# Attention followed by a spatially gated MLP in float32 on one core: fixed PSUM banks for the scores and for the product with v, and one combined wait ahead of each piece

## The chip, the cores and the metric

The kernel runs on one core of one Trainium2 chip. The metric is device time in microseconds (us), lower is better. The profile is of one execution on the same core.

## What is computed

Eight batches of eight heads, 576 positions, head width 64. Attention has a decay between positions, a causal mask and a softmax; its output, with the heads side by side, goes through a gated MLP whose gate mixes the positions.

```python
scores = scale * np.matmul(q, k.transpose(0, 1, 3, 2))          # scale = 1/8
cum = np.cumsum(np.log(np.clip(f, 0.0001, 1.0)), axis=-1)
scores = np.where(causal, -1000000000.0, scores + cum[:, :, :, None] - cum[:, :, None, :])
attn = np.exp(scores - np.max(scores, axis=-1, keepdims=True))
attn = attn / (np.sum(attn, axis=-1, keepdims=True) + 1e-09)
x = np.matmul(attn, v)                                          # then (batch, position, 512)
h = np.maximum(x @ w_in, 0.0)
u, v = h[..., :512], h[..., 512:]
v_n = (v - np.mean(v)) / np.sqrt(np.var(v) + 1e-06)             # mean and variance over the last axis
v_s = np.einsum('ts,bsd->btd', w_spatial, v_n) + b_spatial[None, :, None]
out = (u * v_s) @ w_out
```

## The kernel before, in words

**Attention works on pairs of heads.** There are 32 pairs, four to a batch (`attention`, from L366). For a pair P the matrix engine (PE) does five kinds of work, all of it in float32:

- `scores` (L241): for each block i of 128 query rows, and for each of the two heads h, one product of 64 rows of the array, n = 128(i+1) columns wide, into a PSUM tile `sc`. The two heads lie on partitions 0-63 and 64-127, so that the two products of a block use the two halves of the array's rows. The products are issued in two **pieces** (L246): blocks 2, 1, 0 (L258, called the **small piece** below: widths 384, 256, 128) and block 3 alone (the **wide piece**: width 512). Blocks 0 and 1 of a head share a tile.
- `scores_tail` (L282): the last 64 query rows of both heads, two products of 288 columns (L289, listed under L196, the line of the helper `mm`).
- `transposes` (L320) and `transposes_tail` (L335): the softmaxed rows `tt` and `tl` are turned, 128x128 at a time, into PSUM tiles `tp` (L325 and L336) and copied into `e` alternately by VectorE (DVE) and ScalarE (ACT) (`evac`, L316).
- `attend` (L343): the **product with v**, one piece of 28 matmuls on half of the array's columns each (L352), into two `sc` tiles, x0 and x1.

Every float32 product of L258, L196 (`sc`) and L352 is two instructions in the profile (x2 for one product).

**Between them** DVE adds the decay to the scores, takes the row minimum and writes `tt` (`lowest`, L235, listed under L238); ACT takes the exponential (L271); DVE inverts the row sums (L274, L275); GpSimd (POOL) scales the rows (L279); then they are transposed. `tt` exists once for each head, `tl` once, `e` twice.

**PSUM.** The `sc` tiles come from a pool of four buffers (L521, L535), the `tp` tiles from one of two; two more (`ps`) take the MLP's sums. A new `sc` tile waits for the last reader of the tile that lay there before it.

**What sets the order.** Two Python generators, attention and the MLP of a batch (`moe`, L403), are stepped in turn (L538 to L546), so that the attention of batch b+1 runs beside the MLP of batch b. A scheduler then orders each engine's queue: of the instructions that it holds ready in its own model of time it takes the one with the highest priority. `in_one_piece` (L183) ties the matmuls of a piece together: each after the first has a high priority and an ordering (no semaphore) behind the one ahead of it. The first matmul of a piece is tied to its own tile alone. So the scheduler may start a piece when the first tile is free, and put other matmuls between its members while a later tile is not. Each engine works through its queue strictly in that order.

**The two stages of the run.** Up to about 100 us the weights are loaded and split into two float32r parts (`load64`, L112, on DVE, ACT and POOL) beside the four pairs of batch 0. Then the MLP of batch 0 starts beside pair 4, and so on.

```python
        for piece in ((0, 1, 2), (3,)):
            ...
                    if i == 1:
                        at[i, h] = at[0, h][0], 128
                    else:
                        at[i, h] = PS['s'].tile([128, 512], F32, name="sc"), 0
            ...
            in_one_piece([product(i, h) for i in reversed(piece) for h in range(2)])
```

Of the kernel before, what the change touches and what calls it, by code (L numbers as in the profile page):

```python
# [31 lines left out]
def f32(ap):  # L32
    return ap.bitcast(F32)
# [3 lines left out]
def attn_gmlp_kernel(ctx: ExitStack, tc: tile.TileContext, qk, v, f, w_in, w_sp, b_sp, w_out, out):  # L37
# [141 lines left out]
    def behind(i, j):  # L179
        tc.add_manual_dep(i.ins, j.ins.name, mybir.DependencyInfo(  # L180
            mybir.DependencyClass.NoSync, mybir.DependencyReason.DATA), reason="order")

    def in_one_piece(jobs):  # L183

        was = None
        for n, job in enumerate(jobs):
            if was is None:
                was = job()
            else:
                with tc.high_priority():  # L190
                    i = job()
                behind(i, was)
                was = i

# [40 lines left out]
    def lowest(out, ps, dec, acc_):  # L235
        if len(dec.shape) == 3:
            out, ps = (a.rearrange("p (c w) -> p c w", c=2) for a in (out, ps))
        V.tensor_tensor_reduce(out=out, in0=ps, in1=dec, scale=-0.125, scalar=3.0e38, op0=ALU.add, op1=ALU.min,  # L238
                               accum_out=acc_)

    def scores(P):  # L241
# [4 lines left out]
        for piece in ((0, 1, 2), (3,)):  # L246
            at = {}
            for i in piece:
                for h in range(2):
                    if i == 1:  # L250
                        at[i, h] = at[0, h][0], 128
                    else:
                        at[i, h] = PS['s'].tile([128, 512], F32, name="sc"), 0
# [11 lines left out]
            for i in reversed(piece):  # L265
                for h in range(2):
                    ps, c = at[i, h]
                    n = 128 * (i + 1)
                    t = tt[h][:, TOFF[i]:TOFF[i] + n]
                    lowest(t, ps[:, c:c + n], decay(dk[h], i), nm[h][:, i:i + 1])  # L270
                    last["exp", P, h, i] = A.activation(t, t, AF.Exp, bias=nm[h][:, i:i + 1], scale=-1.0,  # L271
                                                        accum_out=sm[h][:, i:i + 1])
# [9 lines left out]
    def scores_tail(P):  # L282
# [3 lines left out]
        for j in range(2):  # L286
            k0 = 288 * j
            sc = PS['s'].tile([128, 512], F32, name="sc")
            mm(sc[:, 0:288], qk_t[:, TL:640], qk_t[:, 640 + k0:928 + k0], True, True)  # L289
            lowest(tl[:, k0:k0 + 288], sc[:, 0:288], dt[:, k0:k0 + 288], nm[:, j:j + 1])  # L290
            if P == 0:
                keep_warm(6)
            yield 485
        V.tensor_tensor(out=nm[:, 2:3], in0=nm[:, 0:1], in1=nm[:, 1:2], op=ALU.min)
# [21 lines left out]
    def evac(out, ps):  # L316
        (V.tensor_copy if nev[0] % 2 == 1 else A.copy)(out, ps)  # L317
        nev[0] += 1

    def transposes(P, h):  # L320
        for c in range(NB):
# [6 lines left out]
            evac(e_tile(P)[:, h, e0:e0 + n], tp[:, 0:n])  # L328
            yield 107 * (NB - c)

    def transposes_tail(P):
        for cs, off, step in (((4, 3), 576, 640), ((0, 1, 2), 512, 512)):
# [7 lines left out]
            evac(bass.AP(tensor=st.tensor, offset=st.offset,  # L340
# [3 lines left out]
    def attend(P, xh, xl):  # L344

        vt, e = vts[P], es.pop(P)
        x0, x1 = (PS['s'].tile([128, 512], F32, name="sc") for _ in range(2))
# [10 lines left out]
        in_one_piece(jobs)  # L358
        yield 2950
        for ps, s0, n in ((x0, 0, 256), (x1, 256, 320)):  # L360
            last[P, s0 // 256] = A.copy(xh[:, s0:s0 + n], ps[:, 0:n])
            V.tensor_tensor(out=xl[:, s0:s0 + n], in0=ps[:, 0:n], in1=f32(xh[:, s0:s0 + n]), op=ALU.subtract)
# [34 lines left out]
    def acc(b):  # L397

        nps[0] += 1
        pool, tag = ((ps_m, "ps"), (PS["t"], "tp"), (PS["s"], "sc"))[nps[0] % 3 if b == B - 1 else 0]  # L400
# [120 lines left out]
    with tc.tile_pool(name="ws", bufs=2) as ws, tc.tile_pool(name="p0s", bufs=4, space=PSUM) as p0s, \  # L521
# [13 lines left out]
    for k, n in (("s", 4), ("t", 2)):  # L535
# [54 lines left out]
```

## Time and profile before

| | |
|---|---|
| time, median of 3 runs | 825.17 us (824.89 to 825.52) |
| the profiled execution's own time | 830.26 us, its span 828.5 us |
| PE busy | 802.9 us, 97% of the span |
| DVE, ACT, POOL busy | 441.5, 408.2, 387.2 us |
| PE's idle time ahead of L258 in the whole span | 6.6 us |
| PE's idle time ahead of L352 | 2.6 us |
| mean granted PE clock | 0.97 |

A row of a group or of the timeline gives the line, the engine, the operation, what it writes and reads (`sc<-qk_t`), the part of the array (64\*128 is half of the rows, 128\*64 half of the columns) and how many instructions (x4). In the timeline the first number is the start, the second the length; neighbouring matmuls overlap by their pipeline, so what one costs is the distance to the start of the next one.

### The profile page before, as it was taken

The page shows a single profiled execution, that of the slowest core. Times are in us where ns is not written, and L with a number is a line of the kernel's source. Part 1 is how long each engine was busy: PE and PEld are TensorE (multiplying, and loading weights), DVE is VectorE, ACT ScalarE, POOL GpSimd, SP SyncE. Part 2 cuts the span into 40 slices and gives each one's busy share as a digit, 9 for nine tenths or more (in the row PEclk, how much of TensorE's full clock was granted, in tenths as well). Part 3 has the DMA queues.
Part 4 walks back from the last instruction along what each step waited for, and adds up shares of the span by engine and source line. Part 5 has one row for each costly group of instructions (what it writes and reads, how often), then busy time and mean ns, then how long its engine had stood idle before and what let it go on. Part 6 is the DMA issues. An engine that isn't in the chain of part 4 may idle for free.

```text
span 828.5 us, 14548 instructions
## 1 busy us (share of the span) xinstructions
PE 802.9 (97%) x4934; PEld 620.8 (75%) x4934; DVE 441.5 (53%) x1482; ACT 408.2 (49%) x1092; POOL 387.2 (47%) x703
## 2 busy tenths in 40 slices
PE   8888889999999999999999999999999999999997
PEld 3444567877788878887778877888678877888896
DVE  6886687444555546455654446445463445543321
ACT  3565565445654545445554355544454445643321
POOL 4797685443544336444444337344444435432221
PEclk9578899999999999999999999999999999999999
DMA  7563721233222232233212332222222332201001
GB/s 241 174 188 108 218 86 57 82 118 119 76 88 74 85 116 90 93 118 105 74 53 89 102 131 93 87 95 92 72 91 79 118 118 83 61 25 43 26 1 64
DMA packets 35213, 79.44 MB, mean 96 GB/s; under 512 B 4161, under 2 KB 8257, under 8 KB 35138
## 3 DMA queue, kind: packets, MB, share of 16 engines
q1 hardware_dynamic: 34818, 77.98, 29.7%
q8 instruction: 39, 0.64, 0.3%
q10 hardware_dynamic: 320, 0.52, 0.2%
q14 instruction: 36, 0.29, 0.1%
HBM read 68.73 MB, written 9.75 MB: 95 GB/s over the span
## 4 chain that ended last, share of the span: by engine, by line
PE 85%; POOL 1%; issue 0%; DVE 0%; ACT 0%; POOLq 0%
PE ps L196 47%; PE sc L258 11%; PE sc L352 10%; PE tp L325 8%; PE sc L196 5%; PE tp L196 2%; PE tp L336 2%; POOL tt L279 0%; POOL vnl L439 0%; POOL mv L434 0%; POOL w L126 0%; POOL wol L128 0%; ACT o L508 0%; ACT vx L430 0%; DVE st L431 0%
## 5 line engine op out<-in xcount | busy, mean ns | idle before, releaser
L279 POOL TENSOR_SCALAR tt<-tt,sm 128x128 f32<-128x128 f32 (+3 forms) x256 | 134.8, 545 | 154.5 <-DVE sm L275 110.0
L271 ACT ACTIVATE tt<-tt,nm 128x384 f32<-128x384 f32 (+3 forms) x256 | 142.6, 558 | 99.1 <-DVE nm L238 86.6
L258 PE MATMUL sc<-qk_t 64*128 64x128 f32 (+3 forms) x512 | 123.3, 481 | 6.6 <-DVE nm L238 6.3
L325 PE MATMUL tp<-ident,tt 128*128 128x128 f32 x640 | 113.0, 287 | 2.4 <-POOL tt L279 2.4
L317 DVE COPY e<-tp 128x384 f32<-128x384 f32 (+1 forms) x160 | 71.0, 447 | 70.8 <-PE tp L325 56.0
L317 ACT COPY e<-tp 128x256 f32<-128x256 f32 (+1 forms) x160 | 71.4, 450 | 71.8 <-PE tp L325 45.5
L325 PEld LDWEIGHTS tp<-ident,tt 128*128 128x128 f32 x640 | 78.9, 145 | 36.6 <-POOL tt L279 6.7
L484 POOL TENSOR_TENSOR gl<-u,gh 128x256 fp32r<-128x256 f32 (+1 forms) x64 | 51.3, 802 | 107.3 <-ACT gh L483 107.1
L352 PE MATMUL sc<-e,vraw 128*64 128x320 f32 (+4 forms) x896 | 95.4, 365 | 2.6 <-DVE e L317 2.6
L352 PEld LDWEIGHTS sc<-e,vraw 128*64 128x64 f32 x896 | 60.1, 138 | 40.9 <-DVE e L317 4.8
L238 DVE CUSTOM_DVE_ANT_1 tt<-sc,dk 128x256 f32<-128x256 f32 (+1 forms) x128 | 70.3, 552 | 36.6 <-PE sc L258 22.3
L258 PEld LDWEIGHTS sc<-qk_t 64*128 64x128 f32 x512 | 55.0, 191 | 38.8 <-issue 15.2
L196 PE MATMUL ps<-xh,winh 128*128 128x256 f32 (+1 forms) x232 | 74.0, 319 | 2.6 <-ACT vx L430 2.6
L196 PE MATMUL ps<-sph,vnh 128*128 128x256 f32 (+1 forms) x240 | 76.4, 318 | 0.0
L196 PE MATMUL ps<-spl,vnh 128*128 128x256 f32 (+1 forms) x240 | 71.8, 299 | 0.0
L196 PE MATMUL ps<-sph,vnl 128*128 128x256 f32 (+1 forms) x240 | 71.4, 297 | 0.0
L196 PE MATMUL ps<-xl,winh 128*128 128x256 f32 (+1 forms) x232 | 70.7, 305 | 0.0
L196 PE MATMUL ps<-xh,winl 128*128 128x256 f32 (+1 forms) x232 | 70.2, 303 | 0.0
L238 DVE CUSTOM_DVE_ANT_0 tt<-sc,dk 128x128 f32<-128x128 f32 (+1 forms) x128 | 53.4, 419 | 22.5 <-PE sc L258 12.9
L196 PE MATMUL ps<-winh,xh 128*128 128x512 f32 x148 | 61.5, 416 | 0.0
L196 PE MATMUL ps<-winl,xh 128*128 128x512 f32 x148 | 59.5, 402 | 0.0
L483 ACT CAST gh<-u 128x256 fp32r<-128x256 f32 (+1 forms) x64 | 27.6, 433 | 58.1 <-DVE u L480 41.5
(165 smaller groups left out, 1681.7 us busy)
## 6 DMA issues: line engine op xcount, KB each, us to landing
dk<-rows_d SPq DMA_DIRECT2D x64, 320.0 KB, 3.5
qk_t<-in_dram SPq DMA_DIRECT2D x32, 608.0 KB, 3.8
vraw<-in_dram SPq DMA_DIRECT2D x32, 320.0 KB, 3.0
dt<-rows_d SPq DMA_DIRECT2D x64, 144.0 KB, 3.2
out_dram<-o SPq DMA_DIRECT2D x32, 256.0 KB, 2.8
w<-in_dram SPq DMA_DIRECT2D x8, 512.0 KB, 5.8
w<-in_dram SPq DMA_DIRECT2D x8, 256.0 KB, 3.5
wraw<-in_dram SPq DMA_DIRECT2D x4, 288.0 KB, 5.7
```

Source lines behind the costliest of these rows:

```text
L196: T.matmul(o, l, r, start=st, stop=sp)
L238: V.tensor_tensor_reduce(out=out, in0=ps, in1=dec, scale=-0.125, scalar=3.0e38, op0=ALU.add, op1=ALU.min, accum_out=acc_)
L258: return lambda: T.matmul(ps[:, c:c + n], qk_t[p, n - 128:n], qk_t[p, 640:640 + n], start=True, stop=True)
L271: last["exp", P, h, i] = A.activation(t, t, AF.Exp, bias=nm[h][:, i:i + 1], scale=-1.0, accum_out=sm[h][:, i:i + 1])
L279: G.tensor_scalar(out=t, in0=t, scalar1=sm[h][:, i:i + 1], scalar2=1.0, op0=ALU.mult, op1=ALU.mult)
L317: (V.tensor_copy if nev[0] % 2 == 1 else A.copy)(out, ps)
L325: T.transpose(out=tp[:, (i - c) * 128:(i - c + 1) * 128], in_=tt[h][:, TOFF[i] + 128 * c:TOFF[i] + 128 * c + 128], identity=ident)
L336: T.transpose(out=tp[:, j * 128:(j + 1) * 128], in_=tl[:, c * 128:(c + 1) * 128], identity=ident)
L352: return lambda: T.matmul(x[64 * h:64 * h + 64, q0 - s0:q1 - s0], vt[:, c, h, :], e[:, h, e0 + q0:e0 + q1], start=c == 0, stop=c == end)
L483: A.copy(gh[j][:, 0:nt], g)
L484: G.tensor_tensor(out=gl[j][:, 0:nt], in0=g, in1=f32(gh[j][:, 0:nt]), op=ALU.subtract)
```

## The change

Four things are changed.

- **Fixed banks.** The pool of four `sc` buffers becomes four tags, `sc0` to `sc3`, of one buffer each (`bank`). The small piece has banks 0 and 1 for blocks 0 and 1 of the two heads, and banks 2 and 3 for block 2. The wide piece has banks 0 and 1, the tail 2 and 3, the product with v 0 and 1. The MLP of the last batch takes the four in turn.
- **One wait ahead of a piece.** `freed` holds the last reader of each bank. The first matmul of a piece depends, with a semaphore, on the readers of all the banks that the piece has asked for.
- **The product with v** depends besides on all ten copies into `e` of its pair (`copied`), where before each matmul waited for the copies that it reads.
- `lowest` and `evac` return or keep their instructions for this; their work is the same.

The matmuls, their number and their shapes are the same; no instruction is added on DVE, ACT or POOL.

```diff
-    def behind(i, j):
+    def behind(i, j, sync=False):
         tc.add_manual_dep(i.ins, j.ins.name, mybir.DependencyInfo(
-            mybir.DependencyClass.NoSync, mybir.DependencyReason.DATA), reason="order")
-
-    def in_one_piece(jobs):
+            mybir.DependencyClass.Sync if sync else mybir.DependencyClass.NoSync, mybir.DependencyReason.DATA),
+            reason="order")
+
+    freed, banks = {}, []
+
+    def bank(n):
+
+        t = PS['s'].tile([128, 512], F32, name="sc", tag=f"sc{n}")
+        banks.append(n)
+        return t
+
+    def in_one_piece(jobs, needs=()):
 
         was = None
-        for n, job in enumerate(jobs):
+        for job in jobs:
             if was is None:
                 was = job()
+                for j in [freed[n] for n in banks if n in freed] + list(needs):
+                    behind(was, j, sync=True)
             else:
                 with tc.high_priority():
                     i = job()
                 behind(i, was)
                 was = i
+        banks.clear()
...
-                    if i == 1:
-                        at[i, h] = at[0, h][0], 128
-                    else:
-                        at[i, h] = PS['s'].tile([128, 512], F32, name="sc"), 0
+                    at[i, h] = (at[0, h][0], 128) if i == 1 else (bank(i % 3 + h), 0)
...
-                    lowest(t, ps[:, c:c + n], decay(dk[h], i), nm[h][:, i:i + 1])
+                    freed[i % 3 + h if i != 1 else h] = lowest(t, ps[:, c:c + n], decay(dk[h], i), nm[h][:, i:i + 1])
...
-            sc = PS['s'].tile([128, 512], F32, name="sc")
+            sc = bank(2 + j)
             mm(sc[:, 0:288], qk_t[:, TL:640], qk_t[:, 640 + k0:928 + k0], True, True)
-            lowest(tl[:, k0:k0 + 288], sc[:, 0:288], dt[:, k0:k0 + 288], nm[:, j:j + 1])
+            freed[2 + j] = lowest(tl[:, k0:k0 + 288], sc[:, 0:288], dt[:, k0:k0 + 288], nm[:, j:j + 1])
...
-    def evac(out, ps):
-        (V.tensor_copy if nev[0] % 2 == 1 else A.copy)(out, ps)
+    copied = {}
+
+    def evac(P, out, ps):
+        copied.setdefault(P, []).append((V.tensor_copy if nev[0] % 2 == 1 else A.copy)(out, ps))
         nev[0] += 1
...
-        x0, x1 = (PS['s'].tile([128, 512], F32, name="sc") for _ in range(2))
+        x0, x1 = bank(0), bank(1)
...
-        in_one_piece(jobs)
+        in_one_piece(jobs, copied.pop(P))
...
-            V.tensor_tensor(out=xl[:, s0:s0 + n], in0=ps[:, 0:n], in1=f32(xh[:, s0:s0 + n]), op=ALU.subtract)
+            freed[s0 // 256] = V.tensor_tensor(out=xl[:, s0:s0 + n], in0=ps[:, 0:n], in1=f32(xh[:, s0:s0 + n]),
+                                               op=ALU.subtract)
...
-        pool, tag = ((ps_m, "ps"), (PS["t"], "tp"), (PS["s"], "sc"))[nps[0] % 3 if b == B - 1 else 0]
+        k = nps[0] % 3 if b == B - 1 else 0
+        pool, tag = ((ps_m, "ps"), (PS["t"], "tp"), (PS["s"], f"sc{nps[0] // 3 % 4}"))[k]
...
-    for k, n in (("s", 4), ("t", 2)):
+    for k, n in (("s", 1), ("t", 2)):
```

The order of the queues is made anew by the scheduler. Three places of PE's queue show it. In these rows `sc<-qk_t` of widths 384 to 128 is the small piece, of width 512 the wide one, of 288 the tail; `tt_82` and `tt_83` are the rows of the first and the second head, transposed into `tp`; rows of `ps` are the MLP's; x2 are the products of the two heads one behind the other. After the change the helper's line L196 is L208, L258 is L267, L325 is L337, L336 is L348 and L352 is L364.

The first place is the small piece of a pair in the middle of the run. Before:

```order
L258 MATMUL sc<-qk_t 128x384 x2
L258 MATMUL sc<-qk_t 128x256
L196 MATMUL ps<-winh,xl 128x512
L196 MATMUL ps<-winh,xh 128x512
L196 MATMUL ps<-winl,xh 128x512
L196 MATMUL ps<-winh,xl 128x512
L196 MATMUL ps<-winh,xh 128x512
L258 MATMUL sc<-qk_t 128x256
L258 MATMUL sc<-qk_t 128x128 x2
```

The same piece of the changed kernel:

```order
L267 MATMUL sc<-qk_t 128x384 x2
L267 MATMUL sc<-qk_t 128x256 x2
L267 MATMUL sc<-qk_t 128x128 x2
L208 MATMUL ps<-winh,xh 128x512
L208 MATMUL ps<-winl,xh 128x512
L208 MATMUL ps<-winh,xl 128x512
```

The piece is whole: no row of the MLP stands between the 256-wide products of the two heads any more. All small and all wide pieces of the changed kernel stand so.

The second place is the end of a pair, from its last transposes to the product with v. Before, the wide piece of the next pair stands 17 rows ahead of these:

```order
L336 MATMUL tp<-ident,tl 128x128 x2
L196 MATMUL ps<-woh,gl 128x512
L196 MATMUL sc<-qk_t 128x288
L196 MATMUL ps<-woh,gh 128x512
L196 MATMUL ps<-wol,gh 128x512
L196 MATMUL ps<-woh,gl 128x512
L336 MATMUL tp<-ident,tl 128x128 x3
L196 MATMUL ps<-woh,gh 128x512
L196 MATMUL ps<-wol,gh 128x512
L196 MATMUL ps<-woh,gh 128x512
L196 MATMUL ps<-wol,gh 128x512
L325 MATMUL tp<-ident,tt_82 128x128 x4
```

Now:

```order
L267 MATMUL sc<-qk_t 128x512 x2
L337 MATMUL tp<-ident,tt_83 128x128
L348 MATMUL tp<-ident,tl 128x128 x2
L208 MATMUL sc<-qk_t 128x288
L208 MATMUL ps<-woh,gh 128x512
L208 MATMUL ps<-wol,gh 128x512
L208 MATMUL ps<-woh,gh 128x512
L208 MATMUL ps<-wol,gh 128x512
L208 MATMUL ps<-woh,gl 128x512 x2
L348 MATMUL tp<-ident,tl 128x128 x3
L337 MATMUL tp<-ident,tt_82 128x128 x2
```

The wide piece of the next pair has moved back, to ten rows ahead of the first transposes of that same pair (`tt_82`), which need what DVE, ACT and POOL make of it.

The third place is in the first stage, the wide piece of pair 2. Before, with the product with v of pair 1 behind it:

```order
L258 MATMUL sc<-qk_t 128x512
L325 MATMUL tp<-ident,tt_83 128x128 x3
L258 MATMUL sc<-qk_t 128x512
L325 MATMUL tp<-ident,tt_83 128x128 x7
L196 MATMUL sc<-qk_t 128x288 x2
L336 MATMUL tp<-ident,tl 128x128 x5
L352 MATMUL sc<-e,vraw 64x320 x2
```

Now:

```order
L337 MATMUL tp<-ident,tt_83 128x128 x7
L208 MATMUL sc<-qk_t 128x288
L348 MATMUL tp<-ident,tl 128x128 x5
L267 MATMUL sc<-qk_t 128x512 x2
L364 MATMUL sc<-e,vraw 64x320 x2
```

The wide piece is whole and stands behind all transposes of the pair ahead of it; the product with v, which takes the same two banks, follows on its heels.

More of the change, by code (lines that the diff above doesn't have):

```diff
@@ L237, in lowest @@
             out, ps = (a.rearrange("p (c w) -> p c w", c=2) for a in (out, ps))
-        V.tensor_tensor_reduce(out=out, in0=ps, in1=dec, scale=-0.125, scalar=3.0e38, op0=ALU.add, op1=ALU.min,
+        return V.tensor_tensor_reduce(out=out, in0=ps, in1=dec, scale=-0.125, scalar=3.0e38, op0=ALU.add, op1=ALU.min,
                                accum_out=acc_)
@@ L293, in scores_tail @@
             yield 485
+        banks.clear()
         V.tensor_tensor(out=nm[:, 2:3], in0=nm[:, 0:1], in1=nm[:, 1:2], op=ALU.min)
@@ L327, in transposes @@
             e0 = EOFF[c]
-            evac(e_tile(P)[:, h, e0:e0 + n], tp[:, 0:n])
+            evac(P, e_tile(P)[:, h, e0:e0 + n], tp[:, 0:n])
             yield 107 * (NB - c)
@@ L339, in transposes_tail @@
             st = e_tile(P)[:, :, off:off + 64]
-            evac(bass.AP(tensor=st.tensor, offset=st.offset,
+            evac(P, bass.AP(tensor=st.tensor, offset=st.offset,
                          ap=[list(st.ap[0]), [step, n], list(st.ap[1]), list(st.ap[2])]), pv)
@@ L519, in step @@
             return round(done), False
-    with tc.tile_pool(name="ws", bufs=2) as ws, tc.tile_pool(name="p0s", bufs=4, space=PSUM) as p0s, \
+    with tc.tile_pool(name="ws", bufs=2) as ws, tc.tile_pool(name="p0s", bufs=1, space=PSUM) as p0s, \
             tc.tile_pool(name="p0t", bufs=4, space=PSUM) as p0t:
```

## The prediction

> **What bounds the kernel now.** I read the page first, then busy time by stage, the waits of the matrix engine (PE), and PE's timeline around the pieces that the change touches. The page's PE row:
>
> ```profile
> PE 802.9 (97%) x4934; PEld 620.8 (75%) x4934; DVE 441.5 (53%) x1482; ACT 408.2 (49%) x1092; POOL 387.2 (47%) x703
> ```
>
> PE is the only full engine, but 97% is a mean over two stages. Busy time by stretch (PE, weight loads, DVE, ACT, POOL, then PE's granted clock):
>
> ```profile
> 0.00:127.00 127.00, 107.14 (x487) 64.72 (x488) 97.68 (x286) 71.12 (x188) 89.94 (x141) 0.81 0.55 168
> 127.00:826.00 699.00, 695.71 (x4450) 556.12 (x4448) 343.81 (x1197) 337.06 (x904) 297.31 (x562) 1.00 0.26 83
> ```
>
> From 127 us on PE is busy 695.71 of 699 us at full clock: whatever shortens PE's work there shortens the run, as long as nobody makes it wait. Before that PE is idle for 20 us, its clock is 0.81, and the other engines work at the weights. PE's largest waits in the whole run:
>
> ```profile
> PE sc L258 <- DVE nm L238: 6.3, 3, 2.8
> PE sc L196 <- DVE nm L238: 4.0, 3, 1.7
> PE sc L352 <- DVE e L317: 2.6, 3, 1.3
> ```
>
> These waits at PSUM banks and copies, of the kind that the change gathers ahead of each piece, are 13 us together; PE's 3 us of idle time after 127 us can't hold them, so they lie in the first stage. A gain is not to be had from removed waits. It is in the length of the pieces. Two heads of a block use two halves of the array's rows; a whole wide piece (x4) and a whole small piece (x12), each with the row behind it:
>
> ```profile
> 189.64 1.13 PE L258 MATMUL sc<-qk_t 64*128 64x512 f32 x4
> 190.70 0.55 PE L325 MATMUL tp<-ident,tt 128*128 128x128 f32 x3
> ...
> 445.68 1.57 PE L258 MATMUL sc<-qk_t 64*128 64x384 f32 x12
> 447.17 0.55 PE L325 MATMUL tp<-ident,tt 128*128 128x128 f32 x3
> ```
>
> From start to next start a whole wide piece takes 1.06 us, a whole small one 1.49. Now a wide piece that the scheduler has split between its heads:
>
> ```profile
> 400.56 0.39 PE L196 MATMUL ps<-winl,xh 128*128 128x512 f32 x1
> 400.78 0.39 PE L196 MATMUL ps<-winh,xl 128*128 128x512 f32 x1
> 401.10 1.12 PE L258 MATMUL sc<-qk_t 64*128 64x512 f32 x2
> 402.15 0.50 PE L196 MATMUL ps<-winh,xh 128*128 128x512 f32 x1
> 402.49 0.39 PE L196 MATMUL ps<-winl,xh 128*128 128x512 f32 x1
> ...
> 403.74 1.12 PE L258 MATMUL sc<-qk_t 64*128 64x512 f32 x2
> 404.79 0.44 PE L325 MATMUL tp<-ident,tt 128*128 128x128 f32 x2
> ```
>
> One head alone takes 1.05 us, as long as both together. PE never stands idle here, so no view of waits shows it.
>
> **The change part by part: whole pieces.** In the new order every piece is whole. A split wide piece costs 1.05 + 1.05 - 1.06 = 1.04 us too much. Small pieces are split in two ways, into two runs (first four rows) and into three (last six):
>
> ```profile
> 394.41 1.34 PE L258 MATMUL sc<-qk_t 64*128 64x384 f32 x6
> 395.68 0.50 PE L196 MATMUL ps<-winh,xl 128*128 128x512 f32 x1
> ...
> 397.04 0.92 PE L258 MATMUL sc<-qk_t 64*128 64x256 f32 x6
> 397.89 0.33 PE L325 MATMUL tp<-ident,tt 128*128 128x128 f32 x1
> ...
> 420.78 0.92 PE L258 MATMUL sc<-qk_t 64*128 64x384 f32 x4
> 421.63 0.39 PE L196 MATMUL ps<-xh,winl 128*128 128x256 f32 x1
> ...
> 423.38 0.70 PE L258 MATMUL sc<-qk_t 64*128 64x256 f32 x2
> 424.01 0.41 PE L196 MATMUL ps<-xh,winh 128*128 128x320 f32 x1
> ...
> 424.87 0.92 PE L258 MATMUL sc<-qk_t 64*128 64x256 f32 x6
> 425.72 0.55 PE L325 MATMUL tp<-ident,tt 128*128 128x128 f32 x3
> ```
>
> Two runs: 1.27 + 0.85 - 1.49 = 0.63 us too much. Three: 0.85 + 0.63 + 0.85 - 1.49 = 0.84. After 127 us there are 26 pieces of each kind. By the queue of before, 11 wide ones are split, 9 small ones are in two runs and 5 in three: 11 x 1.04 + 9 x 0.63 + 5 x 0.84 = 11.4 + 5.7 + 4.2 = 21.3 us. One row that groups all of L258 in that stage bears it out:
>
> ```profile
> 127.00:826.00 699.00, 93.42 (x416) 42.40 (x416) 1.00 0.26 83
> ```
>
> 416 instructions are 26 pairs of 16. Whole, they would be busy 26 x (1.57 + 1.13) = 70.2 us instead of 93.42.
>
> Each break also makes the array change between halves and whole once more. In the split piece above, rows of the MLP follow each other every 0.22 us; the last one ahead of the piece takes 0.32 (400.78 to 401.10) and the first one behind it 0.34 (402.15 to 402.49): 0.10 and 0.12, here 0.2 together. There are 11 + 9 + 2 x 5 = 30 breaks: 6 us. The Trainium skill ("TensorEngine Tiling (Array Packing)", Key Properties) says that a change of tiling mode drains the engine, and "TensorE: Matmul & The Clock Gate" (step-by-step section of Part 2) gives a drain as about 128 cycles; at 2.4 GHz that makes an estimate of 0.05 us a change, 3 us in all, and the sum below would be 3 us smaller. The rows show twice that, and I go by them. Whole pieces thus bring 27 us, and this is PE's own time at the place that sets the end.
>
> **What the waits add.** No work is added. But what PE waits with now stands ahead of a piece, and everything behind it on PE's queue waits too, the MLP above all. The product with v waits for ten copies and for the readers of banks 0 and 1, the row minima of the next pair's wide piece. In the second stage the new queue puts at least 2.6 us of PE's work between the last transposes of a pair and its product with v, and 6 us between the wide piece and it (worked out from the starts in the timeline of before). That covers a copy (0.55 us, below) and two minima; I cost it at nothing there; without cover it would be some 2 us for a pair.
>
> The nearer danger is the first transposes of the next pair. They need the whole chain behind the wide piece: minimum on DVE, exponential on ACT, inverse, scaling on POOL. At its quickest before:
>
> ```profile
> 259.49 0.55 DVE L317 COPY e<-tp 128x384 f32<-128x384 f32 x1
> ...
> 259.80 1.13 PE L258 MATMUL sc<-qk_t 64*128 64x512 f32 x4
> ...
> 263.02 2.06 POOL L279 TENSOR_SCALAR tt<-tt,sm 128x128 f32<-128x128 f32 x4 [3.39 <-DVE sm L275]
> ```
>
> POOL begins 3.2 us behind the start of the piece; its first two rows are ready at about 3.7 and 4.1. In 11 of 26 pairs the new queue gives only 3.6 us of PE's work before the first two transposes (1.06 for the piece, 0.17 and 0.22 for transposes, 0.48 for the tail, six MLP rows at 0.23, three more transposes 0.33), in 9 pairs 5.4 to 5.9, in 6 pairs 6.4. So 11 pairs stall for about 0.5 us even at the quickest: 5.5 us. At its slowest, with DVE and POOL busy with the MLP's normalisation, the chain takes:
>
> ```profile
> 307.31 1.13 PE L258 MATMUL sc<-qk_t 64*128 64x512 f32 x4
> ...
> 313.28 2.05 POOL L279 TENSOR_SCALAR tt<-tt,sm 128x128 f32<-128x128 f32 x4
> ```
>
> 6.0 us to POOL's start, 6.9 to its second row. If a few pairs meet that I add 2.5 us: 8 us of stalls. The bounds are 0 (the queues of DVE and POOL are made for this order) and 11 x 3.2 + 9 x 1.4 + 6 x 0.4 = 50 us (slow everywhere).
>
> **The first stage.** PE does not set its length: DVE, POOL and the turn-taking of the heads do. POOL's scalings of pair 0 and of pair 4, of which pair 4 has both heads in one row:
>
> ```profile
> 31.06 2.21 POOL L279 TENSOR_SCALAR tt<-tt,sm 128x128 f32<-128x128 f32 x4
> 97.67 4.52 POOL L279 TENSOR_SCALAR tt<-tt,sm 128x128 f32<-128x128 f32 x8
> ```
>
> Four pairs take 66.6 us, 16.7 each. Two things pull apart. A split wide piece at low clock goes away:
>
> ```profile
> 71.09 1.38 PE L258 MATMUL sc<-qk_t 64*128 64x512 f32 x2 [2.77 <-DVE nm L238]
> 72.41 0.69 PE L325 MATMUL tp<-ident,tt 128*128 128x128 f32 x2
> 73.03 2.07 PE L258 MATMUL sc<-qk_t 64*128 64x512 f32 x2
> ```
>
> Up to 2 us for each of two pairs, -4 us. Against that, the wide piece of one head no longer runs ahead of the other head's, and the product with v follows it at once and waits for both its minima, 2 to 3 us for each of three to four pairs: up to +10. I take +3, since the chain of waits in lockstep is the longer term and some of it lies beside POOL's work on weights.
>
> The sum, against the profiled execution's own 830.26 us: -27 + 8 + 3 = -16, 814.3. That execution was 5.1 us above the median of the runs, 825.17; on the median I predict 809.2 us.
>
> **Rivals.** (1) *The full gain*: no stall in the second stage and a first stage of the same length. For it: before, PE has next to no wait in the second stage. Against it: the 3.6 us. The time is 825.2 - 27 = 798. (2) *Most is given back*: stalls of 0.6 us at each of the 26 pairs (16 us) and +9 in the first stage take 25 of the 27 us. For it: the first stage has little to spare on DVE (97.68 of 127 us busy) and POOL (89.94). The time is 823; up to 0.2%, 1.7 us, a measurement of this kernel can't tell from no change. (3) *Slower*: the chain from the wide piece to the next transposes becomes the bound. In the two queues it stood 28 rows ahead of its users before and stands ten rows ahead now (the second place shown above). With a second row ready L us after the piece starts, PE waits 11 x (L - 3.7) + 9 x (L - 5.5); that eats 24 us from L = 5.7 on. At the slow row's 6.9 everywhere it is 50 us: 825.2 - 27 + 50 + 3 = 851. For it: DVE's queue takes copies and normalisation between the two minima; against it: only the pairs like the one at 307.31 were so late, and DVE is busy half the time in this stage. A clock that falls would make it worse:
>
> ```profile
> 70.00:75.00 5.00, 3.90 (x6) 1.09 (x6) 4.25 (x13) 3.05 (x10) 3.94 (x6) 0.68 0.11 25
> ```
>
> This is the stretch of the 2.77 us wait. By this row stalls of 3 us would cost clock as well. The Trainium skill ("TensorE: Matmul & The Clock Gate", Part 1) has the clock halve only after an idle window of about 3.4 us; by that rule the 3.2 us of this rival would cost none.
>
> **How the numbers follow.** I give my forecast (a gain of 8 to 22 us) 0.5, the full gain 0.24, most given back 0.16 (of which a third within 0.2%, two thirds still a little faster), slower 0.10. Faster by over 0.2%: 0.5 + 0.24 + 0.11 = 0.85; within: 0.05; slower: 0.10. The range goes from 797 (full gain, first stage a little shorter) to 821 (stalls 14 us, first stage +9), which leaves out the slower rival and part of the second.
>
> **What would show it.** Right: after the first stage the scores' line (now L267) is busy about 70 us instead of 93, always as x12 and x4; the MLP's rows keep their length; short waits of PE appear at L337 (the transposes) on POOL. Wrong: L267 still in pieces; waits of PE on DVE at L364 or L267 in the second stage of more than 10 us; a first stage longer by over 10 us, seen in the time of the first product of the MLP; a clock below 1.00 after 130 us.

## The result and the profile after

The changed kernel takes 813.7 us (median of 4 runs, 812.37 to 814.74) where the kernel before takes 825.35 us on the same chip (4 runs, 824.89 to 829.19). The ratio is 0.9848 with a 95% interval of 0.9815 to 0.9881: faster by 11.7 us. The profiled execution of the changed kernel took 813.52 us (span 811.7 us), next to its median; that of the kernel before had taken 830.26 us.

Lines below 180 are where they were; L196, L238, L258, L271, L279, L317, L325, L336 and L352 of the kernel before are L208, L250, L267, L280, L288, L329, L337, L348 and L364 of the changed one.

The page's PE row, and busy time by stage (PE, weight loads, DVE, ACT, POOL, then PE's granted clock):

```profile
PE 763.8 (94%) x4933; PEld 606.9 (75%) x4934; DVE 429.4 (53%) x1482; ACT 404.4 (50%) x1092; POOL 382.9 (47%) x703
```

```profile
0.00:127.00 127.00, 88.54 (x475) 54.96 (x476) 93.46 (x279) 68.89 (x183) 83.84 (x135) 0.91 0.52 158
127.00:810.00 683.00, 675.28 (x4460) 551.96 (x4458) 335.89 (x1204) 335.56 (x909) 299.10 (x569) 1.00 0.28 87
```

PE works 39 us less in the whole run, and only 17 us of that shortens the span: the rest has become idle time. PE is still full behind 127 us (675.28 of 683 us, full clock). Ahead of that it is busy for 88.54 us where it was for 107.14, at a clock of 0.91 where it had 0.81, and the stretch is not shorter for it.

The two stages can be parted at the first product of the MLP, which comes right behind the product with v of batch 0's last pair. Its row before, its row after, and the last matmul of the run before and after:

```profile
100.11 0.50 PE L196 MATMUL ps<-winh,xh 128*128 128x512 f32 x1
```

```profile
103.38 0.50 PE L208 MATMUL ps<-winh,xh 128*128 128x512 f32 x1
```

```profile
822.32 0.39 PE L196 MATMUL ps<-woh,gt 128*128 128x512 f32 x1
```

```profile
807.00 0.39 PE L208 MATMUL ps<-woh,gt 128*128 128x512 f32 x1
```

In this pair of profiles the part up to that product is 3.3 us longer, and the rest is 703.6 us where it was 722.2: 18.6 us shorter.

**The pieces behind the first stage.** The scores' line in the stretch that the prediction used, and one whole piece of each kind, of the changed kernel:

```profile
127.00:826.00 699.00, 70.14 (x416) 35.79 (x416) 1.00 0.27 85
```

```profile
260.22 1.13 PE L267 MATMUL sc<-qk_t 64*128 64x512 f32 x4
261.28 0.33 PE L337 MATMUL tp<-ident,tt 128*128 128x128 f32 x1
```

The same 416 instructions are busy for 70.14 us where they were for 93.42: 23.3 us less, at the place that sets the end. A row is shown some 0.07 us longer than the distance to the next start (1.13 against 1.06 us for the wide piece here), and the scores stand in 30 rows fewer (82 before, 52 now); so 21.2 us of it is time won.

**The stall at the next pair's transposes.** The same pair, on PE and on POOL, and then the second of the two transposes and the second of POOL's four scalings alone:

```profile
263.53 0.49 PE L348 MATMUL tp<-ident,tl 128*128 128x128 f32 x3
263.87 0.79 PE L337 MATMUL tp<-ident,tt 128*128 128x128 f32 x2
264.42 0.41 PE L208 MATMUL ps<-sph,vnh 128*128 128x320 f32 x1
```

```profile
263.44 2.07 POOL L288 TENSOR_SCALAR tt<-tt,sm 128x128 f32<-128x128 f32 x4 [3.37 <-DVE sm L284]
```

```profile
264.32 0.33 PE L337 MATMUL tp<-ident,tt 128*128 128x128 f32 x1
```

```profile
263.79 0.48 POOL L288 TENSOR_SCALAR tt<-tt,sm 128x256 f32<-128x256 f32 x1
```

Three transposes of the tail take 0.34 us (263.53 to 263.87), 0.11 each; the second of `tt` starts 0.45 us behind the first. POOL starts to scale 3.2 us behind the start of the wide piece (260.22). The second transpose needs POOL's second row, which ends at 264.27, and starts 0.05 us behind that: it has stalled for 0.34 us. The timeline shows no wait there, since the first transpose is shown 0.33 us long, which covers most of the gap. Such a row of two transposes, 0.78 or 0.79 us long, stands in the second stage 11 times; in the kernel before no row of two is longer than 0.44 us. The 11 stalls are 3.8 us together. The line of the transposes from 127 us on, before and after:

```profile
127.00:826.00 699.00, 93.07 (x540) 64.55 (x540) 1.00 0.26 83
```

```profile
127.00:826.00 699.00, 100.78 (x540) 67.90 (x540) 1.00 0.27 85
```

The same 540 transposes are busy 7.7 us longer. Only a part of that is stalls: they also stand in 221 separate rows where they stood in 193, and a row of one is shown 0.27 us long, a row of two 0.38.

PE's idle time has grown too. From the first product of the MLP to the last matmul, before and after:

```profile
100.10:822.30 722.20, 719.63 (x4571) 575.19 (x4568) 364.88 (x1258) 351.64 (x943) 319.31 (x598) 1.00 0.26 83
```

```profile
103.40:807.00 703.60, 696.04 (x4569) 567.87 (x4568) 354.58 (x1253) 347.76 (x942) 318.62 (x600) 1.00 0.28 86
```

PE stands idle for 7.6 us there where it was 2.6. Of these 5.0 us, 1.3 lie in the 11 stalls.

**The first stage.** PE's largest waits in the whole run:

```profile
PE sc L364 <- ACT tt L280: 7.5, 2, 3.8
PE tp L337 <- POOL tt L288: 6.8, 5, 4.4
PE tp L337 <- ACT e L329: 6.7, 1, 6.7
PE sc L208 <- DVE nm L250: 6.4, 4, 2.7
PE sc L267 <- DVE nm L250: 3.3, 3, 2.0
PE ps L208 <- ACT o L522: 2.5, 5, 1.3
```

The largest single waits of the first three rows, in PE's timeline:

```profile
33.60 2.80 PE L337 MATMUL tp<-ident,tt 128*128 128x128 f32 x10 [4.45 <-POOL tt L288]
...
64.75 2.92 PE L364 MATMUL sc<-e,vraw 128*64 128x320 f32 x28 [3.75 <-ACT tt L280]
...
78.50 0.87 PE L337 MATMUL tp<-ident,tt 128*128 128x128 f32 x3 [6.72 <-ACT e L329]
```

The longest wait of the kernel before was 2.8 us. The waits at banks and copies that the change puts ahead of the pieces are felt here, and next to nowhere else: from 127 us on the largest wait on the list is the last row above, the MLP's.

### The profile page after: what moved, and what is told of

Its sections match the earlier page's. It is cut to its first block, busy times and chain, and to the rows that moved or that the text cites. A ratio compares the mean times of both kernels' runs of the same rounds, so it can differ in the third digit from the quotient of the medians.

```text
span 811.7 us, 14542 instructions
## 1 busy us (share of the span) xinstructions
PE 763.8 (94%) x4933; PEld 606.9 (75%) x4934; DVE 429.4 (53%) x1482; ACT 404.4 (50%) x1092; POOL 382.9 (47%) x703
## 4 chain that ended last, share of the span: by engine, by line
PE 73%; issue 5%; DVE 3%; POOL 2%; DMA 2%; ACT 2%; POOLq 0%; ACTq 0%; DVEq 0%; SPq 0%
PE ps L208 41%; PE sc L364 9%; PE tp L337 8%; PE sc L267 7%; PE sc L208 5%; PE tp L208 2%; DMA out_dram<-o 2%; POOL gl L498 1%; PE tp L348 1%; POOL tt L288 1%; DVE tt L250 1%; ACT tt L280 1%; ACT gh L497 1%; ACT o L522 0%; DVE w L122 0%
## 5 line engine op out<-in xcount | busy, mean ns | idle before, releaser
L288 POOL TENSOR_SCALAR tt<-tt,sm 128x128 f32<-128x128 f32 (+3 forms) x256 | 134.7, 545 | 134.5 <-DVE sm L284 123.8
L280 ACT ACTIVATE tt<-tt,nm 128x384 f32<-128x384 f32 (+3 forms) x256 | 142.7, 558 | 105.6 <-DVE nm L250 103.2
L337 PE MATMUL tp<-ident,tt 128*128 128x128 f32 x640 | 120.4, 287 | 15.7 <-POOL tt L288 6.8
L337 PEld LDWEIGHTS tp<-ident,tt 128*128 128x128 f32 x640 | 81.5, 144 | 54.4 <-issue 15.5
L364 PE MATMUL sc<-e,vraw 128*64 128x320 f32 (+4 forms) x896 | 95.2, 364 | 11.0 <-ACT tt L280 7.5
L250 DVE CUSTOM_DVE_ANT_1 tt<-sc,dk 128x512 f32<-128x512 f32 (+1 forms) x128 | 70.6, 551 | 65.7 <-PE sc L267 45.5
L364 PEld LDWEIGHTS sc<-e,vraw 128*64 128x64 f32 x896 | 61.1, 138 | 48.8 <-ACT tt L280 9.1
L267 PE MATMUL sc<-qk_t 64*128 64x128 f32 (+3 forms) x512 | 87.4, 460 | 3.3 <-DVE nm L250 3.3
L329 ACT COPY e<-tp 128x256 f32<-128x256 f32 (+1 forms) x160 | 72.0, 453 | 36.2 <-PE tp L337 32.6
L329 DVE COPY e<-tp 128x384 f32<-128x384 f32 (+1 forms) x160 | 70.7, 443 | 26.7 <-PE tp L337 19.5
L208 PE MATMUL ps<-xh,winh 128*128 128x256 f32 (+1 forms) x232 | 74.4, 321 | 2.3 <-ACT vx L444 1.5
L208 PE MATMUL ps<-sph,vnh 128*128 128x256 f32 (+1 forms) x240 | 76.1, 317 | 0.3 <-ACT o L522 0.3
L208 PE MATMUL ps<-sph,vnl 128*128 128x256 f32 (+1 forms) x240 | 71.5, 298 | 0.0
L208 PE MATMUL ps<-spl,vnh 128*128 128x256 f32 (+1 forms) x240 | 71.2, 297 | 0.0
L374 DVE TENSOR_TENSOR xl<-sc,xh 128x256 fp32r<-128x256 f32 x64 | 28.4, 454 | 80.9 <-ACT xh L373 80.9
L208 PE MATMUL ps<-xh,winl 128*128 128x256 f32 (+1 forms) x232 | 71.0, 306 | 0.0
L208 PE MATMUL ps<-xl,winh 128*128 128x256 f32 (+1 forms) x232 | 69.4, 299 | 0.0
L250 DVE CUSTOM_DVE_ANT_0 tt<-sc,dk 128x384 f32<-128x384 f32 (+1 forms) x128 | 53.5, 419 | 25.5 <-PE sc L267 14.6
L267 PEld LDWEIGHTS sc<-qk_t 64*128 64x128 f32 x512 | 44.4, 187 | 28.4 <-issue 11.1
L208 PE MATMUL ps<-winh,xh 128*128 128x512 f32 x148 | 62.3, 421 | 2.2 <-ACT o L522 2.2
L208 PE MATMUL ps<-winl,xh 128*128 128x512 f32 x148 | 58.0, 393 | 0.0
```

Of the source, the lines that this page charges most:

```text
L208: T.matmul(o, l, r, start=st, stop=sp)
L250: return V.tensor_tensor_reduce(out=out, in0=ps, in1=dec, scale=-0.125, scalar=3.0e38, op0=ALU.add, op1=ALU.min, accum_out=acc_)
L267: return lambda: T.matmul(ps[:, c:c + n], qk_t[p, n - 128:n], qk_t[p, 640:640 + n], start=True, stop=True)
L288: G.tensor_scalar(out=t, in0=t, scalar1=sm[h][:, i:i + 1], scalar2=1.0, op0=ALU.mult, op1=ALU.mult)
L329: copied.setdefault(P, []).append((V.tensor_copy if nev[0] % 2 == 1 else A.copy)(out, ps))
L337: T.transpose(out=tp[:, (i - c) * 128:(i - c + 1) * 128], in_=tt[h][:, TOFF[i] + 128 * c:TOFF[i] + 128 * c + 128], identity=ident)
```

## The experiments

Each kernel was timed beside the kernel before on its chip. In all of them the pieces behind the first stage are whole, as in the changed kernel, unless something else is said.

**1. The kernel before, profiled again.** No edit.

> The kernel before, unchanged, profiled once more, because its profiled execution (830.26 us) was 5 us above its median. Theory A: that execution was slow in its first stage; a new one takes 823 to 827 us, its first MLP product starts at 94 to 97 us instead of 100.1, and from there to the end it takes the same 722 us; then the change's first stage costs about 8 us and not the 3 that I predicted. Rival B: the profile itself costs 5 us or the second stage varies; then the first MLP product stands at 100 us again.

The profiled run took 826.95 us; 11 timings of the kernel before on that chip gave a median of 826.86 us (821.64 to 833.26). Up to the first product of the MLP, and that product:

```profile
0.00:96.90 96.90, 80.11 (x367) 44.00 (x367) 76.36 (x225) 55.42 (x147) 67.27 (x106) 0.81 0.62 190
```

```profile
96.88 0.50 PE L196 MATMUL ps<-winh,xh 128*128 128x512 f32 x1
```

In the first profile of the same kernel the stretch was 3.2 us longer, at a clock of 0.78:

```profile
0.00:100.10 100.10, 82.81 (x366) 45.65 (x366) 75.93 (x225) 55.47 (x147) 67.94 (x106) 0.78 0.61 187
```

Time by clock is 78.5 and 78.1 us: the same work. From that product to the last matmul both take 722 us. So the two profiles differ by the granted clock of the first stage, and the profile that the prediction was made on had one of the poorest.

**2. The fixed banks alone.** The combined wait is taken out, the one for the copies with it; a piece's first matmul waits for its own tile only.

```diff
-                for j in [freed[n] for n in banks if n in freed] + list(needs):
-                    behind(was, j, sync=True)
```

> The four fixed banks alone, without the combined wait of a piece and without the wait for the copies. In its queue after the first stage all 26 wide pieces are split (11 before), 9 small pieces are in two runs and 4 in three (9 and 5 before). Theory A (a split is what costs): 15 more splits x (1.04 + 0.2) less one of 0.84 + 0.4, about +17 us over the kernel before: 838 to 846 us. Rival B (the fixed banks themselves bring the gain, by freeing tiles in a fixed turn): below 825 us.

848.47 us (4 runs), ratio 1.0267 (1.0216 to 1.0318): slower than the kernel before by 22 us, and 2.5 us above the upper end of theory A. The scores' line from 127 us on:

```profile
127.00:826.00 699.00, 109.19 (x416) 46.52 (x416) 1.00 0.26 81
```

All 26 wide pieces are split in its order, and half of the small ones. The gain is not from the banks; without the wait they do harm. (That it is not the wait for the copies either, run 3 shows.)

**3. No wait for the copies.** The combined wait of a product with v leaves out the copies of the transposes.

```diff
-        in_one_piece(jobs, copied.pop(P))
+        in_one_piece(jobs)
```

> The changed kernel without the wait of the product with v for all copies of its pair; banks and combined waits for banks stay. All pieces are whole as in the changed kernel. Theory A: the copies' wait brings nothing, since the products with v were never split; the second stage is the same within 1 us, and the first stage is 0 to 3 us shorter: 810 to 814 us. Rival B: the copies' wait keeps PE from stalling inside the product with v; without it stalls come back at that line and the time is 815 to 820 us.

813.48 us (6 runs, 810.43 to 815.67), ratio 0.9839 (0.9794 to 0.9884). That is the changed kernel's own time, as theory A had it. In its first stage PE's largest wait is still at the product with v, now named after the readers of the banks:

```profile
PE sc L364 <- DVE nm L250: 9.0, 3, 3.7
PE tp L337 <- ACT e L329: 6.0, 1, 6.0
```

**4. No combined waits in the first stage, fixed banks there.**

```diff
+    def in_one_piece(jobs, needs=(), wait=True):
...
+                for j in [...] + list(needs) if wait else ():
...
+            in_one_piece([product(i, h) for i in reversed(piece) for h in range(2)], wait=P > PPB)
...
+        in_one_piece(jobs, copied.pop(P), wait=P >= PPB)
```

> The changed kernel with the combined waits only after the first stage: scores from pair 5 on, product with v from pair 4 on. After the first stage all pieces are whole. Theory A: the combined wait costs 3 to 8 us in the first stage, where PE has no other work to put in its place; this kernel takes 805 to 811 us, and its first MLP product starts 3 to 8 us ahead of the changed kernel's 103.4. Rival B: the first stage is no slower by the wait (its length is set by DVE and POOL): 812 to 815 us, first MLP product at 102 to 105.

813.89 us (6 runs, 812.9 to 819.66), ratio 0.986 (0.9815 to 0.9906): no gain over the changed kernel, and the first product of the MLP comes at 104.9 us. That is rival B's outcome: with the fixed banks, leaving the waits out of the first stage brings nothing. It does not follow that the waits are free there: runs 8 and 9 show that the fixed banks without them lose as much.

**5. The waits without the fixed banks.** The four banks are handed out in turn, as the pool did.

```diff
-    def bank(n):
+    turn = [0]
+    def bank(_):
+        n = turn[0] % 4
+        turn[0] += 1
...
-                    freed[i % 3 + h if i != 1 else h] = lowest(...)
+                    freed[(r0 + (i % 3 + h if i != 1 else h)) % 4] = lowest(...)
```

> The changed kernel with its combined waits, but with the four banks handed out in turn, as the pool did before, and no longer fixed to the pieces. Theory A (the gain is the waits' alone, since a piece that starts with all its banks free runs whole whichever banks they are): every piece whole, scores' line 70 us after 127 us, time 812 to 816, the changed kernel's own. Theory B (the fixed banks carry a part, since a piece then waits only for banks that were read long ago): pieces whole too, but PE waits ahead of pieces in the second stage for more than the changed kernel's 4 us there, by 5 us or more: 818 to 824.

814.15 us (4 runs, 813.5 to 816.09), ratio 0.9874 (0.986 to 0.9889), and the scores' line is busy for 70.14 us again. Theory A: the gain is the wait's alone, and which bank a piece takes does not matter to it.

**6 and 7. The wait on one kind of piece.** Only the small pieces wait, or only the wide ones; the product with v waits in neither.

```diff
+            in_one_piece([product(i, h) for i in reversed(piece) for h in range(2)], wait=piece != (3,))
...
+        in_one_piece(jobs, wait=False)
```

> Fixed banks, and the combined wait only on the small pieces (the three lower row blocks); the wide pieces and the products with v start as soon as their first bank is free. In the order on PE all 26 wide pieces behind the first stage then run as two halves, all small pieces whole. Theory A (a split costs what two rows of the first profile say: 1.04 us for a wide piece and 0.2 us for the break): 26 x 1.24 = 32 us above the changed kernel, 842 to 848. Theory B (a split costs little by itself, and the gain came from other work moved): below 830.

> Fixed banks, and the combined wait only on the wide pieces. In the order on PE the 26 wide pieces behind the first stage run whole; of the small ones 6 run whole, 6 in two parts and 14 in three. Theory A (the prices of the prediction: 0.63 us and 0.84 us, and 0.2 us for each break): 6 x 0.83 + 14 x 1.24 = 22 us above the changed kernel, 832 to 838; less up to 9 us if the stalls of PE at the next pair's transposes go away, so 825 at the least. Theory B (small pieces cost next to nothing in parts): 812 to 820.

Waits on small pieces alone: 832.5 us (4 runs), ratio 1.0102 (1.0083 to 1.0121). On wide pieces alone: 831.75 us (4 runs), ratio 1.0087 (1.0071 to 1.0104). For run 6 theory A had 842 to 848 and B less than 830, so both missed, A by some 10 us; for run 7 it had 832 to 838, 825 at the least. From 127 us on, the scores' line and the line of the transposes with waits on small pieces alone:

```profile
127.00:826.00 699.00, 99.15 (x416) 43.27 (x416) 1.00 0.25 83
...
127.00:826.00 699.00, 90.34 (x536) 64.08 (x536) 1.00 0.25 83
```

and on wide pieces alone:

```profile
127.00:826.00 699.00, 87.71 (x416) 40.17 (x416) 1.00 0.27 83
...
127.00:826.00 699.00, 98.73 (x540) 66.12 (x540) 1.00 0.27 83
```

With 26 split wide pieces the scores are busy 29.0 us longer than in the changed kernel, 1.12 us a piece; less the 0.07 by which the additional row is shown too long, that is 1.05, next to the prediction's 1.04. From the first product of the MLP to the last matmul the kernel of run 6 takes 725.4 us, 21.8 us more than the changed one. There 27 wide pieces are split, worth 28 us. On the other side PE is idle for 1.9 us instead of 7.6, and none of the 11 stalled rows of two transposes is left. (Of the 10.4 us that the transposes' line is shorter only a part is stalls: they stand in 181 rows instead of 221, and four of them now lie ahead of 127 us.) A split wide piece has other work between its halves, and the next pair's transposes come up late enough for POOL. The price of a split was right; that the waits go away with it had been left out of the expectation. Some 2 us are left for the 27 breaks, less than 0.1 us each, by subtraction alone.

With split small pieces alone the scores are busy 17.6 us longer, 15.2 by distances, where the prediction's prices without the breaks give 15.5. Here the first product of the MLP stands ahead of the product with v of batch 0's last pair, so that the stretch behind it, 729.2 us, holds 28 matmuls more, 2.9 us of work. Without them it is 22.7 us longer than the changed kernel's, of which 1.7 us is a spell of 3.4 us at half clock. The rest, some 6 us, is breaks and waits, which the profile does not part; 5 of the 11 stalled rows remain.

**8. The first stage as before, the second as changed.** The pool of the first stage hands its four buffers out in turn again, and no piece there has the combined wait.

```diff
     def bank(n):
+        if PS['s'].name == "p0s":
+            return PS['s'].tile([128, 512], F32, name="sc")
...
-                for j in [freed[n] for n in banks if n in freed] + list(needs):
+                for j in [freed[n] for n in banks if n in freed] + list(needs) if banks else ():
...
-    with tc.tile_pool(name="p0s", bufs=1, space=PSUM) as p0s, \
+    with tc.tile_pool(name="p0s", bufs=4, space=PSUM) as p0s, \
...
+    freed.clear()
```

> The changed kernel behind the first stage, the kernel before in it: the first stage takes its banks in turn from a pool of four and has no combined waits. All pieces behind the first stage stay whole in the order on PE. Theory A (the waits in the first stage cost what the two profiles say: the first product of the MLP came at 103.4 us with the change and at 96.9 and 100.1 us in two profiles of the kernel before): first product of the MLP at 97 to 100 us, time 808 to 811. Theory B (the end of the first stage is set by its loads and the granted clock, and the difference is spread from run to run): 813 to 815, first product at 102 to 105 us.

804.79 us (5 runs, 803.21 to 805.18), ratio 0.9752 (0.9739 to 0.9766). It beats the kernel before by 20.2 us and, on the same chip, run 5, which takes as long as the changed kernel, by 9.4 us. The time is even below theory A's 808, and the first product of the MLP, at 93.4 us, ahead of its 97. Up to the first product of the MLP:

```profile
0.00:93.40 93.40, 75.87 (x367) 42.82 (x367) 74.67 (x223) 55.32 (x147) 65.92 (x103) 0.84 0.61 192
```

**9. Fixed banks in the first stage, no combined wait there.** As run 8, with the changed kernel's pool and banks: this differs from run 8 in the banks of the first stage alone, and in the order that the scheduler makes of it. The order on PE is that of run 4 throughout.

```diff
-                for j in [freed[n] for n in banks if n in freed] + list(needs):
+                for j in [freed[n] for n in banks if n in freed] + list(needs) if PS["s"].name != "p0s" else ():
...
+    freed.clear()
```

> Beside the kernel that is the kernel before in its first stage and the changed one behind it: only the banks of the first stage are changed, fixed to the pieces as in the changed kernel, but still with no combined wait there. Behind the first stage the order on PE is the same. Theory A (fixed banks without waits split the pieces of the first stage and hold it up as much as the waits do): 811 to 815, first product of the MLP at 100 us or later. Theory B (what made the run with the waits of the first stage left out slow was only the clock granted in it: its first product came at 104.9 us, with 51 us at half clock before it, where 31 us went to half clock in the other kernel): 803 to 808.

813.31 us (5 runs, 812.19 to 815.74), ratio 0.9836 (0.981 to 0.9862). Up to the first product of the MLP:

```profile
0.00:104.60 104.60, 86.11 (x367) 46.01 (x367) 81.22 (x230) 55.80 (x149) 68.83 (x109) 0.76 0.58 182
```

The time is theory A's, and equal to that of run 11 on the same chip, which has the waits. A part of the reason is theory A's too: ahead of this product the scores stand in 18 separate groups in PE's order where run 8 has 14. But the stretch holds 79.5 us at full clock, only 1 us more than run 8's 78.5; most of the difference in this profile is the granted clock, 0.76, as theory B had it. That clock came twice, on two chips (run 4: 104.9 us at 0.76). Run 2 has the same order on PE up to this point and got 97.8 us at 0.83, so fixed banks need not have it.

**10. Run 8 without the wait for the copies.** The edit of run 3 in the kernel of run 8.

> The kernel that is the kernel before in its first stage and the changed one behind it, without the wait for the copies ahead of the products with v. Theory A (the wait for the copies costs nothing and brings nothing, since behind the first stage the copies are long done when a product with v comes up): 803.5 to 806, the same as with it. Theory B (it costs 2 us, the difference of the two profiles behind the first stage, 701.4 against 703.6 us): 802 to 803.5.

808.03 us (6 runs, 803.35 to 810.33), ratio 0.9763 (0.9732 to 0.9794). The median lies above both theories' ranges, and the six timings spread over 7 us. Run 8's 0.9752 lies inside the interval, and a kernel without the wait is not faster: the wait for the copies costs nothing that shows here either. Its first product came at 99.0 us, at a clock of 0.79.

**11. The changed kernel again, beside 9 and 10.**

> The changed kernel once more, beside the others on the same chip: 812 to 815. Theory A (the waits of the first stage cost 13 us there, and the half clock that they spare gives 3 to 7 back): PE idle 15 us or more before the first product of the MLP, which comes at 102 to 107 us. Theory B (the place of the first product is chance): before 100 us in this profile.

813.42 us (5 runs, 812.21 to 813.74), ratio 0.9834 (0.9807 to 0.986). Up to the first product of the MLP PE is busy for 70.11 of 104.3 us:

```profile
0.00:104.30 104.30, 70.11 (x367) 40.30 (x367) 76.75 (x230) 55.76 (x149) 64.57 (x104) 0.85 0.57 177
```

34 us idle, where the kernel before had 17 (80.11 of 96.9, 82.81 of 100.1). Theory A: the place of the first product is not chance.

**The first stage in one table.** The time of the first product of the MLP, the clock granted up to it, and the one multiplied by the other, which is the stretch's length in time at full clock. The clock is rounded, which makes the last column uncertain by 0.5 us:

| banks of the first stage | combined wait there | runs | first product, us | clock | time x clock, us |
|---|---|---|---|---|---|
| in turn | no | before twice, 8, 10 | 100.1, 96.9, 93.4, 99.0 | 0.78, 0.81, 0.84, 0.79 | 78.1, 78.5, 78.5, 78.2 |
| fixed | no | 2, 4, 9 | 97.8, 104.9, 104.6 | 0.83, 0.76, 0.76 | 81.2, 79.7, 79.5 |
| in turn | yes | 5 | 106.5 | 0.87 | 92.7 |
| fixed | yes | after twice, 3 | 103.4, 104.3, 102.5 | 0.88, 0.85, 0.85 | 91.0, 88.7, 87.1 |

With the banks in turn and no waits the last column is the same for four profiles whose first products lie 6.7 us apart: the stretch follows PE's work and the clock. With the fixed banks and no waits it is 1 to 3 us longer. With the waits PE is idle some 17 us more, of which the whole pieces and a better clock give a part back.

## Why the prediction was right, and which term was mis-sized

The forecast was 809.2 us, faster; it is 813.7, faster, within the range. From profile to profile the forecast was 16 us less, and it is 16.7; what is off is the step from there to the median. Step by step:

- *PE bounds the second stage, and the gain is the pieces' length, not removed waits*: right. 70 us were forecast for the scores' line, and it is 70.14. Of the two candidates for the cause, the wait makes the gain (run 5) and the banks do not (run 2).
- *21.3 us for the splits and 6 us for 30 breaks*: the splits were worth 21.2 us (the 23.3 us of the scores' line less 30 rows of 0.07), and run 6 gives the same price for a split wide piece. The breaks were put too high. The stretch behind the first product lost 18.6 us, 1.7 of them a spell at half clock that of the two profiles only that of before has there: 16.9 us. With the 7.5 us of stalls and idle time of the next point that leaves some 3 us for the 30 breaks, 0.1 us each, by subtraction alone.
- *8 us of stalls at the next pair's first transposes, by a chain of 3.7 to 4.1 us against 3.6 us of cover*: the mechanism is shown as forecast, in 11 pairs and at the place forecast, with POOL's start 3.2 us behind the wide piece and a second transpose that starts as soon as POOL's second row is done. The size was not: the 11 stalls are 0.34 us each instead of 0.5, and the 2.5 us for pairs that meet a slow chain did not come. That makes 3.8 us instead of 8. Another 3.7 us of idle time came in that the prediction had put at nothing; in the profile after, 2.5 us of waits at PSUM tiles of the MLP for ACT (L522) is the largest row of it. That the sum, 7.5 us, lies near the forecast 8 is luck. Run 6 bears the mechanism out: with the wide pieces split, none of the 11 is left.
- *No wait for the copies behind the first stage*: right (runs 3 and 10).
- *The rival that is slower*, in which this chain grows to the bound: no pair of the second stage was near it. *The full gain* fails for the 7.5 us and for the first stage.
- *PE does not set the first stage's length*: wrong for the kernel before. Its two profiles, and runs 8 and 10 with the same order there, take 78.1 to 78.5 us at full clock, whatever their length: PE's work and the clock set it.
- *+3 us in the first stage (-4 to +10)*: +3.3 in the two profiles, but mis-sized against the medians. This is the term that failed. The prediction subtracted 5.1 us at the end, because its profile was that much above the median, as if the change kept that difference. Run 1 shows where such a difference lies: half clock in the first stage, which falls on the kernel before because PE's work sets its length there. With the waits PE stands idle in much of that stage, and a poor clock costs less: the changed kernel's five spans of run 11 lie between 810.4 and 812.0 us at mean clocks of 0.973 to 0.982, while the kernel before went from 819.9 us at 0.981 to 831.5 us at 0.968. So against a median execution of the kernel before the first stage costs more than 3 us: 5.4 us by runs 10 and 11 on one chip, 9.4 us by runs 8 and 5 on another. Behind the first stage the change brings about 20 us by the medians (runs 8 and 10 against the kernel before on their chips: 20.2 and 19.6) and 17.0 and 20.4 by their profiles, 19 in the prediction. 20 less 5 to 9 is what was measured, 11.7 to 14.2 us.

These 5 to 9 us can't be put down to the waits alone. With the banks in turn the waits cost them (run 5 against run 8); with the fixed banks the time is the same with the waits (run 11) and without (run 9). Either of the two is enough to lose them.

What stays open is why the fixed banks without waits were granted the poor clock of 0.76 in runs 4 and 9 and not in run 2, and how their unprofiled runs, at mean clocks like run 8's, came out 8 us longer than it. So the clock, which accounts for most of the difference in the profiles, is not shown to be the cause for these two.

## What to carry to other kernels

A wait ahead of a group of matmuls that must run side by side can gain time though no wait goes away, because the scheduler otherwise puts work between two halves that cost as much apart as together; look at start distances, since no view of waits shows it. Use such a wait only where the engine has other work queued ahead: here it is worth some 20 us in the full stage, while in the loading stage the waits, or the fixed banks without them, lose 5 to 9 us. The version with the loading stage left as it was (804.8 us) beats both kernels. A profiled execution's distance from the median belongs to the stage and the mechanism that cause it, and must not be carried over to a kernel that changes that stage.

## What the runs showed of the hardware

The clock of the first stage falls to one half in spells: in the first profile of the kernel before it is 0.50 from 21 to 41 us. Its cost is plain in the table: four first stages of the same order differ by 6.7 us and agree within 0.4 us once multiplied by their clock. The kernel before is at a clock of 0.78 for 100 us, with no wait longer than 2.8 us; the changed kernel waits for up to 6.7 us and gets 0.88. So the length of the single wait does not decide it here, and the prediction's fear that longer stalls would cost clock did not come true for the stage as a whole. The Trainium skill ("TensorE: Matmul & The Clock Gate", Part 1) has the clock halve after an idle window of about 3.4 us; by that rule alone the waits of the kernel before would cost it no clock, and the trace disagrees. The same part of the Trainium skill ("A second HAM failure mode: psum-queue depth-cycling") tells of a kernel whose short idle times between groups of matmuls made the clock swing; the clock of 0.78 beside short waits agrees with that. So the "only" with which the prediction told that rule says more than this part does.
